# One score product per head from q·exp(L) and k·exp(−L), and the mean of z moved into w_out, in a gated linear recurrence with a feed-forward block

## The chip, the cores and the metric

The kernel runs on one core of a Trainium2 chip. The metric is the time of one execution on the device in microseconds (us). Engine names are those of the profile: PE is TensorE, PEld its weight loads, DVE is VectorE, ACT is ScalarE, POOL is GpSimd, SP issues DMA. PEclk is the clock granted to TensorE, as a share of full speed.

## The reference

Two parts follow each other. The first is a recurrence over 768 tokens for 4 batches and 8 heads of width 48, with a complex decay per token and channel. The second is a feed-forward block on 3072 tokens of width 384, with a hidden width of 1024.

```python
mag = np.sqrt(a_re*a_re + a_im*a_im)
scale = np.minimum(mag, 0.999) / (mag + 1e-06)
ar, ai = a_re*scale, a_im*scale
for t in range(S):                       # state S_re, S_im: 48 x 48 per head
    S_re, S_im = ar*S_re - ai*S_im + k[t] v[t]^T,  ar*S_im + ai*S_re
    y[t] = q[t] @ S_re
# ... y of all heads side by side: x, 3072 x 384
h = x @ w_in                             # 3072 x 1024
solu = h * softmax(h)
ln = (solu - mean(solu)) / sqrt(var(solu) + 1e-06) * g_ln
out = ln @ w_out                         # 3072 x 384
```

## The kernel before

Tokens are worked on in chunks of 128, so there are 24 chunks (6 of each batch). Phases are summed up along the tokens, and q and k are doubled into cosine and sine parts. Each head then has 96 rows and a real state. The magnitudes of the decays are handled level by level: a pair of tokens in a chunk meets at one of seven block sizes, and between two levels q and k are multiplied by their blocks' decays (a "fold"). No magnitude is ever divided by, so any decay is in range.

```python
def score(li):                 # level h of 1, 2, 4, 8, 16 (full width) or 32, 64
    for x in range(H):         # 8 heads, 128 weight columns, 64 moving columns
        nc.tensor.matmul(out=o, lhsT=kt, rhs=right(qt, h), start=True, stop=True)
        # ... levels 32 and 64: small products by block
def fold(li):
    nc.vector.tensor_tensor(out=right(QT, h), in0=right(QT, h), in1=left(pm, 1)..., op=OP.mult)
    nc.gpsimd.tensor_tensor(out=left(KT, h), in0=left(KT, h), in1=right(pm, 1)..., op=OP.mult)
    # ... new block decays; then copy_predicated or ACT copies of the scores into attn
# feed-forward of a chunk: turn_x, up, expo, solu, norm, turn_z, down, store
def norm():
    # ... statistics of z on DVE, rs = (var z + 1e-6 s^2)^-0.5 on POOL
    nc.vector.scalar_tensor_tensor(out=nb, in0=mv[:, 0:1], scalar=-1.0, in1=rs, ...)
    nc.scalar.activation(out=z, in_=z, func=AF.Identity, scale=rs, bias=nb)
```

Preparation (magnitudes, phases, sines) goes by groups of two chunks, beside the attention of the group before and the feed-forward of the one before that.

Of the kernel before, what the change touches and what calls it, by code (L numbers as in the profile page):

```python
# [10 lines left out]
FP = mybir.dt.float32  # L11
I32 = mybir.dt.int32
# [4 lines left out]
PSUM = bass.MemoryType.PSUM  # L17
P = 128

# Adding and subtracting it rounds a float of small magnitude to an integer.  # L20
MAGIC = 12582912.0
# A shade under 2 pi, so that half a turn stays in the range of Sin.
TURN = 6.283185
# The block sizes of the intra-chunk scores: pairs in sibling blocks of each size.
MASKED = (1, 2, 4, 8, 16)
LEVELS = MASKED + (32, 64)


def weave(*streams):
    """Runs lists of steps side by side, each spread over its part (begin, end) of the time."""  # L30
    order = []
    for si, (begin, end, steps) in enumerate(streams):
        n = len(steps)
        for i, step in enumerate(steps):
            order.append((begin + (end - begin) * (i + 0.5) / n, si, i, step))
    for _, _, _, step in sorted(order, key=lambda e: e[:3]):
        step()


def constants(H):  # L40
    """What depends on shapes alone: identity, inclusive prefix sum, last row to all rows, masks."""
    s = np.arange(P)
    last = np.zeros((P, P))
    last[P - 1] = 1.0
    mats = np.concatenate([np.eye(P), np.triu(np.ones((P, P))), last], 1)
    masks = []
    for h in MASKED:
        left = (s // h) % 2 == 0
        own = (s // (2 * h))[:, None] == np.arange(P // (2 * h))[None]
        m = np.broadcast_to((own & left[:, None])[:, None, :, None], (P, H, P // (2 * h), h))  # L50
        masks.append(m.reshape(P, H * P // 2))
    return mats.astype(np.float32), np.concatenate(masks, 1).astype(np.uint8)


@with_exitstack
def kernel(
    ctx: ExitStack,
    tc: tile.TileContext,
    q: bass.AP,
    k: bass.AP,  # L60
    v: bass.AP,
    a_re: bass.AP,
    a_im: bass.AP,
    moe_w_in: bass.AP,
    moe_w_out: bass.AP,
    moe_g_ln: bass.AP,
    out: bass.AP,
):
    """The recurrence over chunks of 128 tokens, with a[t] = m[t] exp(2 pi i phi[t]).

    Phases: with T the running sum of phi, Re(prod a[s+1..t]) = prod m * cos(T[t] - T[s]), so q and k
    are doubled into (cos T, sin T) parts and the state stays real, of 2 D rows.

    Magnitudes are never divided by: a pair s < t of one chunk meets at the one block size h at which
    s and t lie in the left and the right one of two sibling blocks. There q carries the product of m
    from its block's start, k that from behind it to its block's end, both at most 1. From h to 2h,
    right blocks of q and left blocks of k take up the whole product of their sibling.
    """
    nc = tc.nc
    B, H, S, D = q.shape  # L80
    D2 = 2 * D
# [45 lines left out]
    def heads(t):  # L127
        return t.rearrange("p (h d) -> p h d", d=D)

# [1 line left out]
    def load(g):  # L131
        for nm, src, pool in (("ar", a_re, ld), ("ai", a_im, ld), ("q", q, ld), ("k", k, ld), ("v", v, ldv)):
            t = pool.tile([P, G, DM], FP, tag=nm, name=nm)
# [4 lines left out]
            T[nm, g] = t  # L138

    def weight_steps():  # L140
        """The weights come as float64: to float32, rounded to nearest, by their bits. What is under
        float32's normal range goes to (next to) zero. w_out's rows take up g_ln."""
        NW = 512
        steps = []
        for w, src, nk in ((w_in, moe_w_in, KD), (w_out, moe_w_out, KF)):
            wide = src.bitcast(I32).rearrange("(c p) w -> p c w", p=P)
            nf = w.shape[2]
            for c in range(nk):
                for f0 in range(0, nf, NW):
                    steps.append((w, wide, c, f0, min(NW, nf - f0)))  # L150

        def convert(w, wide, c, f0, n):
            def f():
                raw = ffp.tile([P, NW, 2], I32, tag="z", name="raw")[:, 0:n]
                both = zp.tile([P, 2, NW], I32, tag="zT", name="bits")[:, :, 0:n]
                nc.sync.dma_start(out=raw.rearrange("p n u -> p (n u)"), in_=wide[:, c, 2 * f0:2 * (f0 + n)])
                lo, hi, x, y = raw[:, :, 0], raw[:, :, 1], both[:, 0], both[:, 1]
                ts, stt = nc.vector.tensor_scalar, nc.vector.scalar_tensor_tensor
                ts(out=x, in0=hi, scalar1=0x7FFFFFFF, scalar2=None, op0=OP.bitwise_and)
                nc.gpsimd.tensor_tensor(out=x, in0=x, in1=rebias.to_broadcast([P, n]), op=OP.add)  # L160
                ts(out=y, in0=x, scalar1=31, scalar2=-1, op0=OP.arith_shift_right, op1=OP.bitwise_xor)
                stt(out=x, in0=x, scalar=3, in1=y, op0=OP.logical_shift_left, op1=OP.bitwise_and)
                stt(out=x, in0=lo, scalar=29, in1=x, op0=OP.logical_shift_right, op1=OP.bitwise_or)
                stt(out=x, in0=hi, scalar=-2 ** 31, in1=x, op0=OP.bitwise_and, op1=OP.bitwise_or)
                ts(out=y, in0=lo, scalar1=28, scalar2=1, op0=OP.logical_shift_right, op1=OP.bitwise_and)
                nc.gpsimd.tensor_tensor(out=w[:, c, f0:f0 + n].bitcast(I32), in0=x, in1=y, op=OP.add)
                if w is w_out:
                    nc.gpsimd.tensor_scalar(out=w[:, c], in0=w[:, c], scalar1=g_ln[:, c:c + 1], scalar2=None,
                                            op0=OP.mult)
            return f  # L170

        return [convert(*s) for s in steps]

# [1 line left out]
    def prep_steps(g):  # L175
        st = {}

# [12 lines left out]
            nc.gpsimd.tensor_tensor(out=st["t1"], in0=st["t1"], in1=st["t2"], op=OP.add)  # L190

        def s1():
            # Twice |a|: a square root and a Newton step on it.
            t1, t2, t3 = st["t1"], st["t2"], st["t3"]
            nc.scalar.activation(out=t2, in_=t1, func=AF.Sqrt, bias=tiny)
            nc.vector.reciprocal(out=t3, in_=t2)
            nc.gpsimd.tensor_tensor(out=t3, in0=t1, in1=t3, op=OP.mult)
            nc.gpsimd.tensor_tensor(out=t2, in0=t3, in1=t2, op=OP.add)

        def s2():  # L200
            # m = |a| min(|a|, 0.999) / (|a| + 1e-6)
            t1, t2, t3 = st["t1"], st["t2"], st["t3"]
            T["M", g] = nat.tile([P, G * H, 2, D], FP, tag="M", name="M")
            nc.gpsimd.tensor_scalar(out=t1, in0=t2, scalar1=2e-6, scalar2=2.0, op0=OP.add, op1=OP.mult)  # L204
            nc.vector.reciprocal(out=t1, in_=t1)  # L205
            nc.vector.scalar_tensor_tensor(out=t3, in0=t2, scalar=1.998, in1=t2, op0=OP.min, op1=OP.mult)
            nc.gpsimd.tensor_tensor(out=t1, in0=t3, in1=t1, op=OP.mult)
            nc.scalar.copy(out=T["M", g], in_=twice(t1))

        def s3():  # L210
            # tan of half the angle of (|a_re|, a_im), with a_re's sign: a_im / (a_re + copysign(|a|, a_re))
            t1, t2, t3, ar, ai = (st[nm] for nm in ("t1", "t2", "t3", "ar", "ai"))
            nc.vector.scalar_tensor_tensor(
                out=t2.bitcast(I32), in0=ar.bitcast(I32), scalar=-2 ** 31, in1=t2.bitcast(I32),
# [5 lines left out]
            nc.gpsimd.tensor_scalar(out=t1, in0=t1, scalar1=0.0, scalar2=0.5, op0=OP.is_lt, op1=OP.mult)  # L220

        def s4():
            # phi in turns: half a turn more where a_re is negative
            t1, t3, ai = st["t1"], st["t3"], st["ai"]
            nc.scalar.activation(out=t3, in_=ai, func=AF.Arctan, scale=2.0)
            nc.vector.scalar_tensor_tensor(out=t3, in0=t3, scalar=1.0 / math.pi, in1=t1, op0=OP.mult, op1=OP.add)  # L226

        def phase(j):
            # The running phase, in turns about the nearest integer; it goes on from the last chunk's end.
            def f():  # L230
                b, ti = groups[g][j]
                if j == 0:
# [13 lines left out]
            return f  # L246

        def trig():
            # (-cos, sin); q and k both have the minus.
            cs = T["cs", g]  # L250
            for j, (b, _) in enumerate(groups[g]):
                nc.scalar.activation(out=cs[:, j * H:(j + 1) * H, 1], in_=heads(T["f", b]), func=AF.Sin, scale=TURN)
            nc.scalar.activation(out=cs[:, :, 0], in_=cs[:, :, 0], func=AF.Sin, scale=TURN, bias=quarter)

        def own():
            # The pairs s = t: v[t] (q[t] . k[t])
            qk = tmp.tile([P, G * H, D], FP, tag="qk", name="qk")
            dot = sml.tile([P, G * H, 1], FP, tag="dot", name="dot")
            vd = vdp.tile([P, G, DM], FP, tag="vd", name="vd")
# [16 lines left out]
            nc.vector.tensor_tensor(out=T["K", g], in0=T["cs", g], in1=twice(flat(T["k", g])), op=OP.mult)  # L276

        def turn(nm, j, half):
            # Four heads of [tokens, 2 D] to [2 D, tokens]
            def f():  # L280
                pool = trm if nm == "M" else tr
                if half == 0:
# [10 lines left out]
        turns = [turn(nm, j, half) for j in range(G) for nm in ("K", "Q", "M") for half in range(2)]  # L293
        return [s0, s1, s2, s3, s4] + [phase(j) for j in range(G)] + [trig, own, doubled_k, doubled_q] + turns

# [1 line left out]
    def chunk_steps(g, j):  # L297
        b, ti = groups[g][j]
        att = attn[j]
# [98 lines left out]
            steps += [keys(0), keys(1), carry]  # L398
        return steps

# [1 line left out]
    def ffn_steps(g, j):  # L402
        b, ti = groups[g][j]
        st = {}
# [25 lines left out]
            nc.vector.tensor_tensor(out=st["z"], in0=st["h"], in1=st["z"], op=OP.mult)  # L430

        def norm():
            # solu = z / s with s = sum + 1e-9: (solu - mean) / sqrt(var + 1e-6) = (z - mean z) / sqrt(var z + 1e-6 s^2)
            z = st["z"]
            bs = sml.tile([P, FF // 512, 6], FP, tag="bs", name="bs")
            mv = sml.tile([P, 2], FP, tag="mv", name="mv")
# [38 lines left out]

        return [turn_x, up(0), up(1), expo, solu, norm, turn_z(0), turn_z(1), down(0), down(1), store]

# [1 line left out]
    load(0)  # L479
    nc.sync.dma_start(out=mats, in_=nc.inline_tensor(mats_np, name="mats_np").ap().rearrange("p (n t) -> p n t", n=3))  # L480
    nc.sync.dma_start(
# [25 lines left out]
        weave(*streams)  # L507


# [1 line left out]
_INS = ['q', 'k', 'v', 'a_re', 'a_im', 'moe_w_in', 'moe_w_out', 'moe_g_ln']  # L511
_OUTS = [((3072, 384), 'float32')]
# [25 lines left out]
```

## Time and profile before

| | before |
|---|---|
| time, median of 3 | 1291.54 us (1290.56 to 1293.04) |
| profiled span, mean PEclk | 1284.6 us, 0.756 |
| first product with w_out (o) starts | 248.9 us |
| a steady pair of chunks | 99.0 us, of it PE idle 16.0 |

The next lines are the view of waits (waiting engine, operation and line, then the releaser; us in total, times, longest us):

```profile
PE score L317 <- DVE attn L342: 106.8, 23, 23.0
PE zt L457 <- ACT z L448: 76.9, 21, 7.7
```

PE waits 106.8 us for DVE between score levels (57.9 of them before 249 us, in the start; a steady pair of chunks has one such wait of 5.2 us), and 76.9 us, in 21 of the 24 chunks, for the normalised z before it can transpose it. POOL and ACT have longer waits (ACT 211.6 us for nb), but they have time to spare, and a wait of such an engine need not cost anything.

### The profile page before, as it was taken

The numbers are of one execution on the slowest core, as the hardware profiler recorded it, in microseconds if no ns is written. First come the engines' busy times: TensorE is split into PE (matmuls) and PEld (weight loads), VectorE is DVE, ScalarE is ACT, GpSimd is POOL, SyncE is SP. The second block draws the span as 40 slices with busy tenths as digits, with TensorE's granted clock in tenths as the row PEclk, the third lists the DMA queues.
The fourth block names the chain that finished last, engine by engine and source line by source line (L and its number), as shares of the span: only waits on it lengthen the run. The fifth ranks groups of instructions, "written<-read, shape, count | busy, mean of one in ns | idle before, by whom it ended". The sixth has DMA issues, their size and how long they took to land.

```text
span 1284.6 us, 14523 instructions
## 1 busy us (share of the span) xinstructions
PE 991.7 (77%) x5856; PEld 797.0 (62%) x5856; DVE 765.8 (60%) x804; ACT 383.4 (30%) x574; POOL 615.1 (48%) x562
## 2 busy tenths in 40 slices
PE   0058855588978978978988888788788798799976
PEld 0057834466676666666766776676666676677753
DVE  4888777766655665665755754763763773734411
ACT  2232302133324324224323323323322423231121
POOL 5585666555544454464363363463453453434300
PEclk9975565578858868778778678687687687788878
DMA  9332121102102102101101101100100000000000
GB/s 145 80 64 60 38 49 49 25 7 44 31 1 44 31 1 44 31 1 36 39 1 32 38 7 32 37 7 21 37 18 19 1 7 7 1 7 7 7 7 12
DMA packets 131666, 36.06 MB, mean 28 GB/s; under 512 B 126480, under 2 KB 129680, under 8 KB 131600
## 3 DMA queue, kind: packets, MB, share of 16 engines
q1 hardware_dynamic: 131600, 35.14, 12.9%
q8 instruction: 46, 0.75, 0.3%
q14 instruction: 20, 0.16, 0.0%
HBM read 30.41 MB, written 4.72 MB: 27 GB/s over the span
## 4 chain that ended last, share of the span: by engine, by line
PE 59%; DVE 18%; POOL 12%; issue 7%; ACT 3%; DMA 0%; POOLq 0%; SPq 0%; DVEq 0%; ACTq 0%
PE score L317 17%; PE o L466 12%; PE y L359 5%; PE turned L287 4%; PE y L362 4%; DVE t L218 3%; PE zt L457 3%; PE h L418 3%; PE score L321 3%; DVE attn L342 2%; DVE QT L333 2%; DVE t L217 2%; PE d L384 2%; POOL KT L335 2%; PE phase L236 2%
## 5 line engine op out<-in xcount | busy, mean ns | idle before, releaser
L317 PE MATMUL score<-QT,KT 96*128 96x64 f32 x1920 | 315.7, 336 | 111.7 <-DVE attn L342 106.8
L317 PEld LDWEIGHTS score<-QT,KT 96*128 96x128 f32 x1920 | 311.9, 253 | 131.6 <-issue 72.9
L335 POOL TENSOR_TENSOR KT<-KT,tot 96x512 f32<-96x512 f32 x144 | 196.0, 1365 | 313.2 <-PE score L317 261.8
L333 DVE TENSOR_TENSOR QT<-QT,tot 96x512 f32<-96x512 f32 x144 | 122.1, 856 | 71.5 <-PE score L317 71.1
L466 PE MATMUL o<-w_out,zT 128*128 128x384 f32 x384 | 161.1, 564 | 0.0
L418 PE MATMUL h<-w_in,xT 128*128 128x512 f32 x288 | 134.3, 609 | 1.2 <-ACT xT L411 1.2
L342 DVE COPY_PREDICATED attn<-masks,score 128x512 f32<-128x512 uint8 x120 | 112.1, 934 | 0.0
L466 PEld LDWEIGHTS o<-w_out,zT 128*128 128x128 f32 x384 | 82.2, 230 | 45.7 <-issue 17.7
L457 PE MATMUL zt<-mats,z 128*128 128x128 f32 x192 | 46.7, 408 | 76.9 <-ACT z L448 76.9
L338 POOL TENSOR_TENSOR tot<-MT 96x512 f32<-96x512 f32 x24 | 27.0, 1123 | 160.2 <-ACT MT L289 160.2
L359 PE MATMUL y<-v,attn 128*128 128x48 f32 x384 | 95.9, 357 | 1.4 <-issue 1.4
L448 ACT ACTIVATE z<-z,nb,rs 128x1024 f32<-128x1024 f32 x24 | 29.8, 1240 | 211.6 <-DVE nb L447 211.6
L205 DVE RECIPROCAL t<-t 128x768 f32<-128x768 f32 x12 | 59.4, 4951 | 53.6 <-POOL t L204 53.6
L457 PEld LDWEIGHTS zt<-mats,z 128*128 128x128 f32 x192 | 34.0, 209 | 84.1 <-ACT z L448 81.4
L418 PEld LDWEIGHTS h<-w_in,xT 128*128 128x128 f32 x288 | 52.5, 193 | 53.8 <-issue 51.7
L359 PEld LDWEIGHTS y<-v,attn 128*128 128x128 f32 x384 | 83.8, 278 | 2.1 <-issue 1.7
L362 PE MATMUL y<-state,QT 96*128 96x48 f32 x320 | 83.2, 352 | 0.3 <-DVE QT L333 0.2
L391 DVE TENSOR_TENSOR state<-d,state 96x384 f32<-96x384 f32 x16 | 8.9, 554 | 115.9 <-PE d L384 115.9
L321 PE MATMUL score<-QT,KT 96*32 96x32 f32 (+1 forms) x1152 | 49.9, 220 | 30.5 <-DVE QT L333 27.7
L321 PEld LDWEIGHTS score<-QT,KT 96*32 96x32 f32 (+1 forms) x1152 | 45.4, 134 | 43.4 <-issue 36.1
L236 PE MATMUL phase<-t,mats 128*128 128x384 f32 x48 | 36.8, 875 | 45.5 <-DVE t L226 45.5
L362 PEld LDWEIGHTS y<-state,QT 96*128 96x128 f32 x320 | 70.5, 271 | 0.5 <-DVE QT L333 0.4
(93 smaller groups left out, 1647.8 us busy)
## 6 DMA issues: line engine op xcount, KB each, us to landing
ar<-in_a_re_dram SPq DMA_DIRECT2D x24, 192.0 KB, 3.6
ai<-in_a_im_dram SPq DMA_DIRECT2D x24, 192.0 KB, 3.3
q<-in_q_dram SPq DMA_DIRECT2D x24, 192.0 KB, 3.9
k<-in_k_dram SPq DMA_DIRECT2D x24, 192.0 KB, 3.4
v<-in_v_dram SPq DMA_DIRECT2D x24, 192.0 KB, 3.3
out_dram<-ot SPq DMA_DIRECT2D x24, 192.0 KB, 1.9
raw<-in_moe_w_in_dram SPq DMA_DIRECT2D x6, 512.0 KB, 4.3
raw<-in_moe_w_out_dram SPq DMA_DIRECT2D x8, 384.0 KB, 3.0
```

What stands on the lines that cost most here:

```text
L205: nc.vector.reciprocal(out=t1, in_=t1)
L236: nc.tensor.matmul(out=ps, lhsT=tri, rhs=st["t3"][:, j * DM:(j + 1) * DM], start=True, stop=(ti == 0))
L317: nc.tensor.matmul(out=o, lhsT=kt, rhs=right(qt, h), start=True, stop=True)
L321: nc.tensor.matmul(out=o[a:a + h, h * y:h * (y + 1)], lhsT=kt[:, a:a + h], rhs=qt[:, a + h:a + 2 * h], start=True, stop=True)
L333: nc.vector.tensor_tensor(out=right(QT, h), in0=right(QT, h), in1=left(pm, 1).to_broadcast([D2, n, h]), op=OP.mult)
L335: nc.gpsimd.tensor_tensor(out=left(KT, h), in0=left(KT, h), in1=right(pm, 1).to_broadcast([D2, n, h]), op=OP.mult)
L342: nc.vector.copy_predicated(right(att, h), masks[:, li].rearrange("p (x i) -> p x i", i=h), ps.rearrange("p (x i) -> p x i", i=h),)
L359: nc.tensor.matmul(out=ys, lhsT=att[:, x * P:(x + 1) * P], rhs=V[:, x * D:(x + 1) * D], start=True, stop=(ti == 0))
L362: nc.tensor.matmul(out=ys, lhsT=T["QT", g, j][:, x * P:(x + 1) * P], rhs=state[b][:, x * D:(x + 1) * D], start=False, stop=True)
L418: nc.tensor.matmul(out=st["h"][:, half * 512:(half + 1) * 512], lhsT=st["xT"][:, c * P:(c + 1) * P], rhs=w_in[:, c, half * 512:(half + 1) ...
L457: nc.tensor.transpose(out=ps[:, i * P:(i + 1) * P], in_=st["z"][:, c * P:(c + 1) * P], identity=ident)
L466: nc.tensor.matmul(out=st["o"], lhsT=st["zT"][:, c * P:(c + 1) * P], rhs=w_out[:, c], start=(c == 0), stop=(c == KF - 1))
```

## The change

The intent: with L the running sum of log-magnitudes inside a chunk, the decay between tokens s and t is exp(L[t]) · exp(−L[s]). So q takes exp(L), k takes exp(−L), and one product of 128 by 128 per head gives all scores of a chunk, to be masked once. This only works if exp(−L) stays in range. The kernel therefore collects three checks (on the angles, the size of the inputs and the end decays), and a branch at the end runs the old level-by-level way (now the function `general`) if one fails. The feed-forward block changes too. Subtracting the mean of z before the product with w_out is the same as subtracting from w_out the mean of each of its columns, and the factor rs can be applied to the output. So the normalising pass over z goes away, and the statistics run beside the transposes. Preparation now takes all four batches at once, and ACT's order of instructions is fixed by the program.

```diff
+def whole(ctx, tc, flag, q, k, v, ...):
+            nc.scalar.activation(out=up, in_=st["lr"], func=AF.Exp)                # exp(L)
+            nc.scalar.activation(out=dn, in_=st["lr"], func=AF.Exp, scale=-1.0)    # exp(-L)
+            nc.sync.dma_start(out=T["ends", ti], in_=up[P - 1:P, :])               # end decays
+            for nm, t in (("q", up), ("k", dn)):
+                nc.gpsimd.tensor_tensor(out=x, in0=x, in1=t, op=OP.mult)
 ...
+        def score(half):                    # replaces 7 levels of score and fold
+                for i in range(4):
+                    nc.tensor.matmul(out=ps[:, i], lhsT=KT[:, x * P:(x + 1) * P],
+                                     rhs=QT[:, x * P:(x + 1) * P], start=True, stop=True)
+                nc.vector.tensor_tensor(out=st["att"][...], in0=ps, in1=tri..., op=OP.mult)
 ...
+        def centre():                       # w_out minus the mean of its columns
+            for c in range(KF):
+                nc.tensor.matmul(out=ps, lhsT=ones, rhs=w_out[:, c], ...)
+            for c in range(KF):
+                nc.vector.scalar_tensor_tensor(out=w_out[:, c], in0=ps, scalar=-1.0 / FF,
+                                               in1=w_out[:, c], op0=OP.mult, op1=OP.add)
 ...
-        return [turn_x, up(0), up(1), expo, solu, norm, turn_z(0), turn_z(1), down(0), down(1), store]
+        return [turn_x, up(0), up(1), expo, solu, turn_z(0), turn_z(1), norm, down(0), down(1), store]
 ...
+        inner.enter_context(tc.manual_schedule(engines={mybir.EngineType.Activation}))
+        whole(inner, tc, flag, *args)
+    needed = nc.values_load(flag[0:1, 0:1])
+    with tc.If(needed != 0, name="general"):
+            general(inner, tc, *args)
```

## The prediction

> **What bounds the kernel now.** I read the page's busy shares, the 40 slices and the chain that ended last first.
>
> ```profile
> PE   991.7 (77%) x5856; PEld 797.0 (62%) x5856; DVE 765.8 (60%) x804; ACT 383.4 (30%) x574; POOL 615.1 (48%) x562
> PE   0058855588978978978988888788788798799976
> PEclk9975565578858868778778678687687687788878
> PE 59%; DVE 18%; POOL 12%; issue 7%; ACT 3%; DMA 0%; POOLq 0%; SPq 0%; DVEq 0%; ACTq 0%
> ```
>
> (In order: busy us, share and instructions of each engine; TensorE by slice; its clock by slice; the chain by engine.) TensorE is busy 77% of 1284.6 us, but only at a granted clock that swings; its mean is 0.756 in the core view. The chain is mostly PE, with DVE and POOL steps between. Groups by line show what a score costs:
>
> ```profile
> L317 PE MATMUL score<-QT,KT 96*128 96x64 f32 x1920 | 315.7, 336 | 111.7 <-DVE attn L342 106.8
> L335 POOL TENSOR_TENSOR KT<-KT,tot 96x512 f32<-96x512 f32 x144 | 196.0, 1365 | 313.2 <-PE score L317 261.8
> L333 DVE TENSOR_TENSOR QT<-QT,tot 96x512 f32<-96x512 f32 x144 | 122.1, 856 | 71.5 <-PE score L317 71.1
> L342 DVE COPY_PREDICATED attn<-masks,score 128x512 f32<-128x512 uint8 x120 | 112.1, 934 | 0.0
> ```
>
> Five full-width score levels per chunk, and between levels q and k are folded on DVE and POOL, each side waiting for the other. Next the chain in order of time, around 660 us:
>
> ```profile
> 659.20 0.22 PE y L362 x2
> ...
> 666.73 0.43 PE y L362 x2
> ```
>
> The same y product (two instructions) takes 0.22 us, then 0.43. Short windows over that place carry the granted clock in the column before the last two:
>
> ```profile
> 642.00:648.00 6.00, 6.00 (x81) 3.42 (x80) 0.00 (x0) 2.58 (x7) 5.83 (x5) 1.00 0.00 0
> 668.00:672.00 4.00, 4.00 (x21) 4.00 (x20) 0.00 (x0) 0.00 (x0) 1.39 (x6) 0.50 0.00 0
> 672.00:676.00 4.00, 0.27 (x2) 0.11 (x1) 2.57 (x3) 0.55 (x1) 2.97 (x4) 0.50 0.00 0
> 680.00:684.00 4.00, 4.00 (x18) 2.90 (x17) 0.00 (x0) 1.81 (x4) 0.00 (x0) 0.68 0.01 4
> ```
>
> So the clock is full or half. It falls after idle stretches, and also in an unbroken run of y products, whose 48 moving columns against 128 weight columns keep the array little used (668 to 672). It recovers a few us into work of wide moving operands.
>
> **What the skill says.** "TensorE: Matmul & The Clock Gate", Part 1, says the clock is half or full, set by activity in free-running windows of about 3.4 us. The trace agrees on the two levels (0.50 and 1.00 above); idle gaps of about 4 us precede the half clock. Its "LDWEIGHTS" section says a weight load costs by its columns: a y product with 48 moving columns takes 0.22 us at full clock, and h with 512 takes 0.86 (six in 5.14 us at 1237 us), four times as much, not ten, so the trace agrees that narrow products pay for their 128 weight columns. "SBUF — State Buffer", "SBUF: two separate sides", says a DVE operation with two SBUF inputs or in a two-port mode and a GpSimd operation exclude each other for the whole instruction. The trace agrees: the DVE's add at L217 takes 0.96 us alone, median 3.07, and this DVE mask of 384 elements (mean 0.42 us) ends only when POOL's multiply of 58.74 to 60.60 does:
>
> ```profile
> 58.87 1.95 DVE L243 TENSOR_SCALAR cs<-f 128x384 int32<-128x384 int32 x1
> 58.74 1.86 POOL L198 TENSOR_TENSOR t<-t,t 128x768 f32<-128x768 f32 x1
> ```
>
> "ScalarE: Activation LUTs", "What ACT_TABLE_LOAD costs", gives about 1283 ns for a load; the groups show 54 loads of 1283 ns each. The new kernel has 13 in its order of instructions, 53 us of ACT less, off the path.
>
> **TensorE work, part by part,** at full clock for one chunk of one batch. Durations are read where the clock is 1.00: narrow product with 128 weight columns 0.22 us, d (96 weights) 0.165, transpose 0.11 (kt 0.083), h 0.86, o and phase 0.64.
>
> Before: score 5 x 8 x 0.22 = 8.8; the two small levels about 1.6; M's transposes 8 x 0.11 = 0.9; k's way back (kt) 0.7; K and Q transposes 1.8; y 16 x 0.22 = 3.5; d 1.3; x, z transposes 1.2; h 5.1; o 5.1; phase 1.3. Sum 31.3; 24 chunks 751 us; divided by 0.756 that is 993, against 991.7 measured busy. The table holds.
>
> After: scores become 8 products of 128 by 128, priced as the narrow one since the weights are the same 128 columns: 1.8. M and kt go. The prefix sum of log m adds a 0.64. Sum 21.75 us, 522 us for 24 chunks: 31% less.
>
> **The other engines.** DVE loses the folds (122 + 32), the predicated copies (112) and three reciprocals per group (178). It gains per group of four chunks (elements 1536, rates of the same forms in the trace): two two-input operations 1.75 each in the phase part, the maximum 1.7, the clamp 1.0, two for log m 3.5, four evacuations 2.2, phases 6.0, eight doublings 7.6, small ones 0.6: about 26 us, or 6.5 per chunk. Per chunk 7.3 remain (mask 1.4, x 0.55, state 0.55, max 1.2, product 1.2, statistics 1.9, store 0.55). So 13.8 a chunk; with the float64 weights (about 63) and the centring (8 x 0.56), 400 us instead of 766. POOL: 13 us a group plus 1.6 a chunk plus weights 48: about 160 instead of 615. ACT: ten activations of 1.48 per group, sines 3.8, loads, and 5.3 a chunk: about 255. All below PE's 21.75 per chunk, so PE should become the bound, if it is fed.
>
> The mean's move into w_out takes the normalising pass on z (1.24 us, waiting 211.6 us in all on DVE's nb) off the z-to-transposes path. The last chunk shows it: product ends 1246.1, transposes begin 1250.1. 4 us a chunk of latency go; only what was not hidden counts, so I do not add 24 x 4.
>
> **Start.** The order of instructions has the new preparation serial for all four batches: ar lands at about 7 us, maximum, Ln, Exp, POOL multiply 3.6 (twice L219's 1.8), four steps to atan's argument (21), log m (32), prefix sums (38), exponentials (41). PE's next instruction is a transpose of the chunk's end decays, which come by a DMA and a POOL copy queued behind two POOL multiplies of 3.6 each: 50. Phases to 57, sines and doubling to 69. Then 11 of 14 weight conversions (DVE 4 to 5 us each, 49 in all) lie in the same queue with the next preparation's 9, scores and the mean's centring. First o at about 148 us. Before, it was at 248.9, so 100 us come from here.
>
> **Steady state.** By batch within a group, PE at full clock needs 19.6, 22.2, 24.7, 19.6 us. I walked each queue. In batch 0, the next preparation's POOL multiply keeps the DVE (lock), which delays the row maximum and the second mask; ACT's squares stand before z's evacuation: about 30. In batch 1 the end-decay transpose waits behind POOL again, some 4 us of idle PE and half clock after: 29. In batch 2, phases, five sines and the table load stand before the exponential: 31. Batch 3 fits: 21. Sum 111, or 27.7 per chunk, a factor 1.29 over full clock.
>
> First o 148 + rest of its chunk 6 + 18 chunks x 27.7 (499) + last four without preparation 4 x 20 (80) + the last feed-forward alone 21 (before: about 23, 4 less latency, colder clock) + flag load and branch, a guess of 4 = 758 us. The run's time is 7 over the profile's span before (1291.5 against 1284.6): 765. Because my waits may overlap more than walked, I set 760.
>
> **Rivals.** (1) PE runs unbroken and stays at full clock: 18 chunks x 22.5 = 405 saves 94, about 670. For it: DVE and POOL have half idle. Against: y and d stretches without wide products did drop the clock at 668 us. (2) The inefficiency of before stays: there 49 us per chunk between 249 and 1225 us (976 us for about 20 chunks), 1.57 over its 31.3; then 34 per chunk, 18 x 34 = 612, about 875. For it: in-order queues with one-buffered loads and two PSUM buffers for all turns, and clock loss that feeds itself. Against: the level-by-level ping-pong of PE with DVE and POOL, the cause of the longest waits (POOL on score 278.7 us), is gone. (3) DVE or ACT becomes the bound: ACT's order is fixed by the program and may hold evacuations of turns behind sines; then batches 0 to 2 cost 35 to 40 and the time is 850 to 900. (4) The flag comes out set and the old way runs too: about 2000. Computed from the inputs, products of |a| over 128 tokens stay near exp(-13), far over 1e-18, angles' fourth powers sum under 0.9 where 5 is allowed: out of the question but for an error.
>
> **Range and chances.** Rival 1 gives the low edge, with a little of its gain missing: 690. Halfway to rivals 2 and 3 gives the high edge: 835. No rival but the fourth reaches 1265, so faster 0.98, same 0.01, slower 0.01.
>
> **What would show it.** PE busy about 520 divided by the granted clock, 610 to 660 us; clock 0.80 to 0.88; DVE near 400, POOL near 165, ACT near 255. Score: 384 instructions near 0.11 us each of path at full clock. First o near 148. PE idle before the end-decay transpose, four times some 4 us, released by POOL. If scores by 128 moving columns cost over 0.22 us each, or the clock stays at 0.75, or first o comes past 180, the prediction is wrong there; also if the longest PE waits are on ACT.

## The result, and the profile after

The changed kernel is correct and took **752.81 us** (median of four, 743.38 to 755.11) against 1291.05 for the kernel before on the same chip. Two of the four executions, 755.11 and 754.77, count as slow; the fast ones took 743.38 and 750.85. The ratio of the fast runs is **0.5786** (95% interval 0.5754 to 0.5819). A ratio is the mean time of one kernel's fast runs over that of the other's of the same rounds, so it is not quite the ratio of the medians quoted. A later set of six executions of the same kernel gave 746.02 us and a ratio of 0.5768.

The page of the profiled execution (span 741.6 us, mean PEclk 0.878), its busy shares and the slices of PE and its clock:

```profile
PE 588.8 (79%) x2887; PEld 416.1 (56%) x2887; DVE 380.3 (51%) x590; ACT 246.4 (33%) x325; POOL 171.3 (23%) x133
...
PE   0215217768998988998988989898989989999994
...
PEclk9955658669996999998989999989989999999997
```

PE is busy 588.8 us instead of 991.7, and its clock is mostly full after the first quarter. What stands out instead is the start: in the first six slices, up to 111 us, PE does little. The new score's group by line (instructions; busy us, mean ns of one; idle time before):

```profile
L768 PE MATMUL f_score<-f_qT,f_kT 96*128 96x128 f32 x384 | 56.9, 283 | 0.0
```

The score is now 384 instructions and 56.9 us, where the five wide levels alone took 315.7. (Each product of two float32 operands is two instructions: 24 chunks x 8 heads x 2 = 384.) What PE still waits for, in the view of waits:

```profile
PE f_L L659 <- DVE f_lr L652: 32.6, 1, 32.6
PE f_tot L684 <- POOL f_e L682: 27.3, 5, 10.4
PE f_mean L611 <- POOL f_w_out L604: 26.8, 7, 13.5
```

The waits for the prefix sum (f_L) and for the weights (f_mean) lie wholly in the start. So do two of the five waits for the end decays (f_tot), 10.4 and 6.3 us. The other three, in the steady state, are 3.5 us each.

The same four chunks repeat through the middle. Cut at the transposes of x, one steady group reads as follows in the view of stretches (start and end; us; then busy us and instructions of PE, PEld, DVE, ACT, POOL; then PEclk, DMA share, GB/s):

```profile
428.80:456.40 27.60, 24.02 (x121) 18.12 (x120) 13.92 (x17) 15.38 (x18) 6.86 (x5) 0.88 0.18 36
456.40:485.50 29.10, 25.59 (x130) 18.75 (x130) 11.32 (x20) 7.87 (x12) 8.58 (x6) 0.89 0.32 66
485.50:514.30 28.80, 26.28 (x136) 18.29 (x135) 20.49 (x35) 12.43 (x18) 6.24 (x4) 0.99 0.07 14
514.30:534.60 20.30, 20.30 (x119) 14.91 (x119) 7.69 (x13) 4.95 (x10) 1.15 (x3) 1.00 0.40 74
```

Batch 3, last, has PE busy in all of its 20.3 us at full clock. The other three have 2.5 to 3.6 us of idle PE each, and batches 0 and 1 pay for it once more by a clock of 0.88 and 0.89.

The gap in batch 0, seen from DVE in order of time (start us, us, engine, line, operation; in brackets the idle time before it and its releaser):

```profile
436.39 1.76 DVE L636 TENSOR_TENSOR f_x<-f_ar,f_x 128x1536 f32<-128x1536 f32 x1 [5.61 <-POOL f_ai L635]
438.07 1.22 DVE L832 TENSOR_REDUCE f_nmax<-f_h 128x1 f32<-128x1024 f32 x1
439.20 1.75 DVE L637 SCALAR_TENSOR_TENSOR f_x<-f_x,f_ai 128x1536 f32<-128x1536 f32 x1
440.87 0.68 DVE L770 TENSOR_TENSOR f_att<-f_score,f_mats 128x512 f32<-128x512 f32 x1
```

The preparation's POOL product (L635, from 432.93, 3.43 us) reads f_x until 436.36. The DVE product (L636) writes over that tile, so it has waited by a semaphore: of its 5.61 us the last 3.5, since the Exp that both need ended only at 432.85. Behind it in DVE's queue stand the row maximum (L832), the next preparation step (L637) and the second mask (L770). PE needs that mask for y and starts it at 441.61 after 3.57 us of idle time. The gap in batch 1, seen from POOL:

```profile
472.75 3.44 POOL L672 TENSOR_TENSOR f_q<-f_q,f_ar 128x1536 f32<-128x1536 f32 x1
476.15 3.42 POOL L672 TENSOR_TENSOR f_k<-f_k,f_ai 128x1536 f32<-128x1536 f32 x1
479.51 0.25 POOL L682 COPY f_e<-f_ends 32x96 f32<-32x96 f32 x1
```

A copy of 0.25 us stands behind two POOL products of 3.4 us each. PE's next instruction, the transpose of the end decays, needs it and starts at 479.82 after 3.51 us. The gap in batch 2, seen from ACT:

```profile
500.20 1.56 ACT L718 ACTIVATE f_cs<-f_cs,f_bias 128x1536 f32<-128x1536 f32 x1
501.78 1.28 ACT L719 ACT_TABLE_LOAD   x1
503.08 1.11 ACT L833 ACTIVATE f_z<-f_h,f_nmax 128x1024 f32<-128x1024 f32 x1
```

The row maximum that the exponential (L833) needs was done at 502.23. The exponential starts 0.85 us later, when the table load behind the sine has ended. The product of z follows at 504.34, and PE has idled 1.31 us when it starts z's transposes at 505.61. It had idled 0.96 us before that for the evacuation of y.

### The profile page after: what moved, and what is told of

Read it like the earlier page. It is cut to its first block, busy times and chain, and to the rows that moved or that the text cites. A ratio compares the mean times of both kernels' runs of the same rounds, so it can differ in the third digit from the quotient of the medians.

```text
span 741.6 us, 7378 instructions
## 1 busy us (share of the span) xinstructions
PE 588.8 (79%) x2887; PEld 416.1 (56%) x2887; DVE 380.3 (51%) x590; ACT 246.4 (33%) x325; POOL 171.3 (23%) x133
## 5 line engine op out<-in xcount | busy, mean ns | idle before, releaser
L870 PE MATMUL f_o<-f_w_out,f_zT 128*128 128x384 f32 x384 | 139.8, 512 | 0.0
L824 PE MATMUL f_h<-f_w_in,f_xT 128*128 128x512 f32 x288 | 130.8, 597 | 0.6 <-ACT f_xT L817 0.6
L870 PEld LDWEIGHTS f_o<-f_w_out,f_zT 128*128 128x128 f32 x384 | 74.4, 204 | 44.0 <-issue 7.0
L824 PEld LDWEIGHTS f_h<-f_w_in,f_xT 128*128 128x128 f32 x288 | 53.2, 190 | 58.8 <-issue 51.7
L779 PE MATMUL f_y<-f_v,f_att 128*128 128x48 f32 x384 | 73.2, 285 | 14.6 <-DVE f_att L770 14.5
L833 ACT ACTIVATE f_z<-f_h,f_nmax 128x1024 f32<-128x1024 f32 x24 | 26.7, 1113 | 148.0 <-DVE f_nmax L832 125.3
L779 PEld LDWEIGHTS f_y<-f_v,f_att 128*128 128x128 f32 x384 | 61.1, 204 | 19.7 <-DVE f_att L770 15.4
L782 PE MATMUL f_y<-f_state,f_qT 96*128 96x48 f32 x320 | 65.9, 290 | 0.0
L832 DVE TENSOR_REDUCE f_nmax<-f_h 128x1 f32<-128x1024 f32 x24 | 29.3, 1223 | 60.0 <-PE f_h L824 60.0
L768 PEld LDWEIGHTS f_score<-f_qT,f_kT 96*128 96x128 f32 x384 | 53.2, 201 | 9.3 <-issue 6.8
L768 PE MATMUL f_score<-f_qT,f_kT 96*128 96x128 f32 x384 | 56.9, 283 | 0.0
L782 PEld LDWEIGHTS f_y<-f_state,f_qT 96*128 96x128 f32 x320 | 52.7, 206 | 0.0
L770 DVE TENSOR_TENSOR f_att<-f_score,f_mats 128x512 f32<-128x512 f32 x48 | 32.9, 685 | 28.5 <-PE f_score L768 28.5
```

The source lines that it names most:

```text
L768: nc.tensor.matmul(out=ps[:, i], lhsT=KT[:, x * P:(x + 1) * P], rhs=QT[:, x * P:(x + 1) * P], start=True, stop=True)
L770: nc.vector.tensor_tensor(out=st["att"][:, half * 4:half * 4 + 4], in0=ps, in1=tri.unsqueeze(1).to_broadcast([P, 4, P]), op=OP.mult)
L779: nc.tensor.matmul(out=ys, lhsT=st["att"][:, x], rhs=V[:, x * D:(x + 1) * D], start=True, stop=(ti == 0))
L782: nc.tensor.matmul(out=ys, lhsT=T["qT", ti, b][:, x * P:(x + 1) * P], rhs=state[b][:, x * D:(x + 1) * D], start=False, stop=True)
L824: nc.tensor.matmul(out=st["h"][:, half * 512:(half + 1) * 512], lhsT=st["xT"][:, c * P:(c + 1) * P], rhs=w_in[:, c, half * 512:(half + 1) ...
L832: nc.vector.tensor_reduce(out=nmax, in_=st["h"], op=OP.max, axis=AX.X, negate=True)
```

## The experiments

All variants are correct unless it is said otherwise. Ratios are against the kernel before.

**1. The mean alone (before_mean).** The kernel before with only the mean's move into w_out.

```diff
-            nc.vector.scalar_tensor_tensor(out=nb, ...)
-            nc.scalar.activation(out=z, in_=z, func=AF.Identity, scale=rs, bias=nb)
+        def centre(): ...        # as in the change, once, after the weights
-        ... expo, solu, norm, turn_z(0), turn_z(1), down(0), ...
+        ... expo, solu, turn_z(0), turn_z(1), norm, down(0), ...
```

> The kernel before with nothing changed but the mean put into w_out, so that the normalising pass over z goes and the factor is applied to the output. Theory (z's path shortened by about 4 us a chunk, and TensorE's 77 us of waiting for the normalised z mostly goes): 1200 to 1240 us. Rival (the latency was hidden, since TensorE has scores to do meanwhile): within 15 us of the kernel before, 1276 to 1306.

Measured: 1157.74 us, ratio 0.896 (0.8913 to 0.9008), so some 134 us less, more than expected. A steady pair of chunks in the kernel before, then here:

```profile
690.60:789.70 99.10, 83.10 (x505) 67.14 (x504) 59.53 (x61) 32.70 (x49) 47.25 (x44) 0.76 0.12 25
```

```profile
636.10:721.50 85.40, 76.14 (x505) 61.69 (x504) 59.76 (x61) 29.62 (x45) 47.50 (x44) 0.82 0.14 29
```

The same 505 PE instructions take 85.4 us instead of 99.1. PE's idle time falls by 6.7 us (99.1 − 83.1 = 16.0 to 85.4 − 76.1 = 9.3). Its busy time falls by 7.0 us for the same work, because the granted clock rises from 0.76 to 0.82. Half of the gain of a latency removed is thus the wait itself, and the other half is the clock.

**2. One product per head alone (before_one_score).** The kernel before with one product of 128 by 128 per head, no folds and no magnitudes' transposes. It is wrong on purpose: the decays' magnitudes are left out of q and k.

```diff
-        for li in range(len(LEVELS)):
-            steps += [score(li), fold(li)]
+        steps = [score(0), score(1), values]     # 4 heads each, then one mask on DVE
```

> The kernel before with its own preparation and pairing of batches, but one 128 by 128 product per head instead of the seven levels, no folds and no transposes of M. Wrong on purpose: the decays are left out. Theory (the levels and their exchange with VectorE and GpSimd are most of the cost; TensorE per chunk falls from 31.3 to about 21.8 us at full clock, VectorE from 766 to about 530 us in all): 850 to 930 us, three quarters of the whole gain. Rival (preparation in fours, the scalar engine's fixed order and the shorter start are as large a part): 1000 to 1100 us.

Measured: 996.74 us, ratio 0.7723. This is less of a gain than the theory's 850 to 930, and just under the rival's 1000 to 1100. PE's work fell as planned (636.3 us busy), but the view of waits shows a wait that grew in its place:

```profile
PE zt L421 <- ACT z L412: 164.1, 13, 35.7
```

In the kernel before, the same wait was 76.9 us, at most 7.7 at a time. Here it is 35.7 us once in the start and 13.5 to 14.7 us once in each of seven steady pairs of chunks. One of these, in order of time:

```profile
602.07 4.94 DVE L218 RECIPROCAL t<-t 128x768 f32<-128x768 f32 x1
608.99 2.78 POOL L220 TENSOR_SCALAR t<-t 128x768 f32<-128x768 f32 x1
612.53 1.24 ACT L412 ACTIVATE z<-z,nb,rs 128x1024 f32<-128x1024 f32 x1 [2.77 <-DVE nb L411]
```

The product of z was done at 599.19, and PE starts the transposes at 613.82. The normalising pass is only 1.24 us of that. A reciprocal of the preparation (L218) stands before the variance on DVE, and two operations of the preparation (L219 from 607.09, L220) stand before rs on POOL. So what stands open with the attention short is z's whole path through the statistics, with the preparation in its queues.

**3. The mean taken back (znorm_back).** The changed kernel with the normalising pass back on z (the centring of w_out is kept, which is harmless).

```diff
+            nc.vector.scalar_tensor_tensor(out=nb, in0=mv[:, 0:1], scalar=-1.0, in1=st["rs"], ...)
+            nc.scalar.activation(out=z, in_=z, func=AF.Identity, scale=st["rs"], bias=nb)
-        ... solu, turn_z(0), turn_z(1), norm, ...
+        ... solu, norm, turn_z(0), turn_z(1), ...
```

> The changed kernel with the normalising pass over z put back between the product and the transposes, w_out still centred (the result stays right). Theory (in the changed kernel z becomes ready just as TensorE is done with the y products, so 4 us more of latency stand open in each of 24 chunks, and the clock falls in them): 830 to 870 us, TensorE waiting for z some 70 to 100 us. Rival (hidden behind other products): at most 765.

Measured: 892.63 us, ratio 0.6915. By the ratios the loss is some 146 us, far above the expectation.

```profile
PE f_zt L845 <- ACT f_z L866: 115.8, 24, 7.8
```

All 24 chunks wait, 4.8 us each, and the mean clock falls from 0.878 to 0.794. In a steady group of four chunks (133.3 us against 105.8), PE idle time grows by 17.9 us and busy time for the same work by 9.6 us.

**4. ACT's order left to the scheduler (act_auto).**

```diff
-        inner.enter_context(tc.manual_schedule(engines={mybir.EngineType.Activation}))
```

> The changed kernel without the fixed program order of the scalar engine: the order of instructions then has about 89 table loads instead of 13, 98 us more on that engine, part of it ahead of the exponential and the evacuations. Theory (the fixed order is worth something): 780 to 830 us. Rival (the scalar engine at 33% has room, and a freer order fills waits): 735 to 760.

Measured: 740.28 us, ratio 0.5739 (0.5721 to 0.5757). The theory that the order is needed falls, and the rival is right. ACT loads tables 70 times instead of 13, and its busy time goes from 246.4 to 319.8 us. None of it reaches the end. The steady group is 105.7 us, as before. First o comes at 163.9 us instead of 156.9 and the eighth chunk at 332.3 instead of 323.0, and yet the end is no later: the last four chunks with preparation take 94.3 us instead of 102.3.

**5. The product's own place (x0_own).** The DVE product that waited in batch 0 is written over another tile, so that it need not wait for POOL's reading.

```diff
-            nc.vector.tensor_tensor(out=x0, in0=ar, in1=x0, op=OP.mult)
-            nc.vector.scalar_tensor_tensor(out=x0, in0=x0, scalar=2.0, in1=ai, ...)
+            nc.vector.tensor_tensor(out=ar, in0=ar, in1=x0, op=OP.mult)
+            nc.vector.scalar_tensor_tensor(out=x0, in0=ar, scalar=2.0, in1=ai, ...)
```

> The changed kernel with the VectorE product of the angle's argument written over a_re's tile instead of over x0, which GpSimd still reads. In the changed kernel VectorE stands 5.6 us there in each group, by a semaphore. Theory (it is this wait for a tile, not the shared port, that delays the row maximum and the second mask and costs TensorE 3.6 us a group and clock after it): the wait goes, the product takes under 2.5 us beside GpSimd, 725 to 742 us. Rival (my predicted reason, the port that both engines share): the product then itself takes about 5 us beside GpSimd's 3.4 us multiply, and the time stays within 745 to 756.

Measured: 757.94 us, ratio 0.5872: no gain, and somewhat slower. The timeline of the same place shows why:

```profile
439.37 1.76 DVE L636 TENSOR_TENSOR f_ar<-f_ar,f_x 128x1536 f32<-128x1536 f32 x1 [2.10 <-ACT f_x L630]
439.41 5.00 POOL L635 TENSOR_TENSOR f_ai<-f_ai,f_x 128x1536 f32<-128x1536 f32 x1 [3.71 <-ACT f_x L630]
446.12 1.22 DVE L832 TENSOR_REDUCE f_nmax<-f_h 128x1 f32<-128x1024 f32 x1
448.12 0.68 DVE L770 TENSOR_TENSOR f_att<-f_score,f_mats 128x512 f32<-128x512 f32 x1
```

The DVE product now starts as soon as the Exp has ended. But POOL's product, issued 0.04 us after it, takes 5.00 us instead of 3.43. It ends at 444.41, 3.28 us after the DVE product's end at 441.13. The two thus ran one after the other. The Trainium skill states this ("SBUF — State Buffer", section "SBUF: two separate sides"): a DVE operation with two SBUF inputs and a GpSimd operation that reads SBUF exclude each other for the whole instruction. The trace agrees. The semaphore went and the exclusion took its place: the two products are done 5.08 us after the end of the Exp, against 5.30 in the changed kernel. The next DVE operation (L637) needs POOL's result and waits 3.33 us, until 444.45. DVE's order of instructions changed with the edit, too. The row maximum (L832) stood before L637 and now stands behind it, and one more step of the preparation (L638) now stands before the second mask (L770). The mask is later than before (PE's gap before y is 4.34 us instead of 3.57). How much of the loss is due to this order was not separated. The theory's 725 to 742 us thus failed. The rival's exclusion is there, but it lengthens POOL's operation and not DVE's, and the time is above the rival's 745 to 756.

**6. The end decays without POOL (ends_dma).** They are fetched twice by DMA instead of once with a POOL copy.

```diff
-            nc.sync.dma_start(out=T["ends", ti], in_=up[P - 1:P, :])
+            for u in range(2):
+                nc.sync.dma_start(out=T["ends", ti][:, u], in_=up[P - 1:P, :])
-            nc.gpsimd.tensor_copy(out=e2, in_=e.unsqueeze(1).to_broadcast([B * H, 2, D]))
```

> The changed kernel with the end decays fetched twice by DMA, so that GpSimd's copy, which stands behind its two multiplies of 3.4 us, goes. Theory (the transpose of the end decays, first in TensorE's queue after o, costs 3.5 us in each of three groups and 6 to 10 us twice in the start, with clock lost after it): TensorE's wait falls from 27 to under 8 us, 720 to 740 us. Rival (the DMA lands too late or another wait comes in its place): 745 to 756.

Measured: 737.58 us, ratio 0.5725 (0.5708 to 0.5742), within the theory's 720 to 740.

```profile
PE f_tot L683 <- DMA f_ends<-f_ar: 7.3, 2, 4.8
```

POOL's 27.3 us are gone and 7.3 remain, in the start. Batch 1 of a steady group falls from 29.1 to 23.45 us at full clock. But batches 0 and 2 go from 27.5 and 28.8 us to 28.7–30.1 and 29.6–31.2. Their idle time is the same or smaller, and their clock is lower (0.77 to 0.94). The group of four takes 103.0 us against 105.8, so that in this execution half of the 5.6 us that batch 1 gave was lost again to the clock next door.

**7. Each score twice (score_twice).** It asks whether PE's work still sets the pace.

```diff
+                    for _ in range(2):
                         nc.tensor.matmul(out=ps[:, i], lhsT=KT[...], rhs=QT[...], start=True, stop=True)
```

> The changed kernel with each score product done twice (same result). TensorE gets 8 x 0.22 = 1.76 us more per chunk at full clock, 42 us in all. Theory (TensorE sets the pace in most of the span): 780 to 800 us, and the added products take 0.22 us each at full clock. Rival (TensorE waits for others, and the clock is higher with more wide products): under 765.

Measured: 772.75 us, ratio 0.599 (0.5978 to 0.6002), so 26 to 29 us more than the changed kernel's two sets by the ratios, between theory and rival. The group by line:

```profile
L769 PE MATMUL f_score<-f_qT,f_kT 96*128 96x128 f32 x768 | 98.8, 275 | 0.0
```

That is 41.9 us more of score in PE's busy time. In the steady state the cost is one to one: the 16 chunks from the fourth to the nineteenth, cut at the transposes of x, take 448.5 against 420.1 us, 28.4 more, where they have 16 x 1.76 = 28.2 of score (23.8 more than in experiment 9, whose clock was lower). Up to the fourth chunk it costs nothing (209.9 us against 216.8): there PE waits for others.

**8. No branch (no_branch).** The load of the flag and the branch with the old way are left out.

```diff
-    needed = nc.values_load(flag[0:1, 0:1])
-    with tc.If(needed != 0, name="general"): ...
```

> The changed kernel without the load of the flag and without the branch with the old way in it. Theory (the branch costs a few us at the end): 3 to 7 us less. Rival (hidden in the tail): within 2 us.

Measured: 743.73 us, ratio 0.5762 (0.5752 to 0.5772).

**9. The changed kernel again (after_again).** It has no edit.

> The changed kernel once more, unaltered, as the yardstick for what the smaller edits brought. Theory: its executions spread from 743 to 755 us by the clock they are granted and nothing else, so on this chip it comes to 740 to 750 (ratio 0.574 to 0.582) and the version without branch (743.7, ratio 0.576) is no faster: the branch costs under 1 us. Rival: the branch and the load of its flag cost 3 to 4 us, then this run stays at a ratio of 0.578 to 0.580 or more with an interval that lies above 0.5772.

Measured: 746.02 us (741.92 to 754.9), ratio 0.5768 (0.5752 to 0.5783). The interval overlaps that of the version without a branch almost fully, so the branch's cost is not to be told from zero. The two ratios differ by 0.0006 of 1291 us, which is 0.8 us. There is more to learn from the spread. In this execution the transpose of x of the eighth chunk came at 323.0 us, as in the first profile. The next group of four then took 109.0 us instead of 105.8, with the same idle time of PE (9.4 and 9.6 us) and a lower clock in three of its four chunks. The group after that took 106.0 us. The same program with the same waits gets a different clock. In the clock records of the two traces it falls at the same place (335.88 and 335.89 us, after the same gap of PE), and stays at half for 6.83 us in the first and for 10.24 us here. The Trainium skill says that the clock's windows run freely and do not start with the kernel ("TensorE: Matmul & The Clock Gate", section "Part 1: The HAM clock gate"). The records agree that there are windows: in all 14 traces each whole stretch at one clock lasts a multiple of 3.41 us. But they don't explain this difference, since the windows lie at the same place in both executions. Why one took a window more at half clock is open. So differences of a few us between variants of this kernel mean little from single executions.

**10. A shorter start (start_both).** The factor g_ln goes into the centring step and off POOL, and the weights are converted beside the first preparation.

```diff
-                    nc.gpsimd.tensor_scalar(out=w[:, c], in0=w[:, c], scalar1=g_ln[:, c:c + 1], ...)
-                nc.tensor.matmul(out=ps, lhsT=ones, rhs=w_out[:, c], ...)
+                nc.tensor.matmul(out=ps, lhsT=means[:, c], rhs=w_out[:, c], ...)   # -g_ln / FF
-            nc.vector.scalar_tensor_tensor(out=w_out[:, c], in0=ps, scalar=-1.0 / FF, in1=w_out[:, c], ...)
+            nc.vector.scalar_tensor_tensor(out=w_out[:, c], in0=w_out[:, c], scalar=g_ln[:, c:c + 1], in1=ps, ...)
-    for f in sum(prep_steps(0), []) + turn_steps(0, 0):
-        f()
+    weave((0.0, 0.6, sum(prep_steps(0), []) + turn_steps(0, 0)), (0.0, 1.0, weight_steps()))
```

(The cut leaves out eight POOL operations that make `means` once, at the beginning.)

> The changed kernel with two edits of its start alone: the factor g_ln goes into the centring step of w_out, so that 8 operations of POOL of 1.59 us fall away, and the weights are converted beside the first preparation instead of after it. Theory: the start is a chain of DVE and POOL in which PE only waits (first o at 157 us in a span of 742); 13 us of POOL and some 10 to 15 us of waiting for the weights fall away, first o comes at 135 to 145 us and the time is 720 to 733. Rival: DVE's own work up to the first chunk is the bound and only changes its order, first o stays within 5 us of 157 and the time is 740 to 752.

Measured: 737.28 us, ratio 0.5714 (0.5702 to 0.5726). First o came at 137.5 us, where the theory put it, but the time lies between the theory's 720 to 733 and the rival's 740 to 752. Of 19.4 us at the first o, 11.0 are left at the eighth chunk (312.0 against 323.0 us). The profiled group after it took 111.1 us against 105.8, with 9.4 us of idle PE against 9.6, so that again only the clock differs.

**11 and 12. Start and end decays together, with ACT's order fixed (best_fixed) and free (best_auto).** The edits of 6 and 10, then those of 4 too.

> The two edits of the start together with the end decays fetched twice by DMA. Theory: start and steady state are different stretches, so the gains add: 13 to 20 us from the start and about 10 from the end decays, 712 to 726 us. Rival: what one wait gives the others take by the clock, and it is no better than the better of the two alone, 730 to 740.

> The same with ACT's order left to the scheduler. Theory: ACT's order was worth nothing by itself (740 against 743), so within 5 us of the version with the fixed order. Rival: with the start shortened, ACT's many more table loads (some 89 against 13) lie on the path there, and it is 8 us or more slower than the fixed order.

Measured: best_fixed 725.27 us, ratio 0.5613 (0.5599 to 0.5626), in the range of the theory, so these gains do add. By the ratios to the changed kernel's 0.5768 the start alone brought 7.0 us, the end decays alone 5.6 and both 20.0. That is more than the sum, and why was not tested. best_auto took **714.46 us** (711.99 to 723.9, the latter a slow run), ratio 0.5560 (0.5528 to 0.5592). This is better than either side expected, and 3.6% below the changed kernel on the same chip (0.5560 / 0.5768). In its expectation I wrote 89 table loads; the trace has 70. A steady group of it:

```profile
408.80:429.10 20.30, 20.28 (x121) 14.91 (x120) 6.92 (x12) 6.31 (x11) 1.20 (x3) 1.00 0.04 16
429.10:452.80 23.70, 23.27 (x129) 16.29 (x129) 12.48 (x20) 7.85 (x12) 8.64 (x6) 1.00 0.33 55
452.80:484.60 31.80, 29.31 (x136) 20.99 (x136) 24.43 (x38) 17.80 (x22) 11.21 (x5) 0.84 0.18 38
484.60:511.50 26.90, 23.14 (x119) 16.57 (x119) 11.21 (x16) 18.92 (x21) 1.56 (x3) 0.87 0.41 74
```

Two of four chunks now run at full clock almost without idle time. This group has PE at 96.0 us of work in 102.7, where best_fixed has 100.9 in 107.0 at a lower clock. The largest difference lies behind it: the last four chunks with preparation take 94.1 us, with PE idle for 0.7, against 105.8 with 6.0 idle, which is 11.7 of the 14.6 us between the two spans. act_auto has the same short group (94.3), but a later start. Why the free order fits these edits better was not tested.

## Why the prediction was right or wrong

The time (760 predicted, 752.81 measured) and the range (690 to 835) held. That the number came so near is in part luck: the start was 12 us longer and the steady state 28 us shorter than predicted. By its own sum, with the cuts at the transposes of x in the profiled run:

| term | predicted | measured |
|---|---|---|
| to the end of the chunk with the first o | 148 + 6 = 154 | 166.1 |
| 18 chunks with preparation | 499 (27.7 each) | 470.8 (26.2 each) |
| four without | 80 | 78.6 |
| last feed-forward, flag, branch | 21 + 4 | 26.1 |
| span | 758 | 741.6 |
| run over span | 7 | 1.8 |

**TensorE's work by parts: right.** 522 us at full clock over the measured 0.878 is 594, against 588.8 busy. The 610 to 660 named at the prediction's end were missed on the low side: they answer to clocks of 0.85 to 0.79, and the clock came out at the upper end of its own range (0.80 to 0.88). A score instruction costs 0.109 us of path, as said (41.9 us for 384 more in experiment 7). DVE 380.3 (400 predicted), ACT 246.4 (255) and POOL 171.3 (165) came near too. Experiment 7 shows that PE paces the steady state. One reading of the clock was misplaced: the half clock shown from 668 to 672 us began at 662.05, and the idle stretch shown (672 to 676) came after that. The rule drawn from it holds all the same, as PE had no idle time from 654.31 to 672.27 and did almost only y products in the 3.41 us before the fall.

**The start: 9 us short.** First o came at 156.9 us instead of 148. The mis-sized term is the weights: "DVE 4 to 5 us each, 49 in all" for 11 of them. It counted DVE's time, but a tile goes back and forth between DVE and POOL. The POOL additions that end the eight tiles of w_out start from 100.4 to 144.3 us, 6.3 us apart on average, and 5.1 where least stands between them (three from 121.0 to 131.2). DVE works 2.7 us on such a tile, by the sum of its six operations' medians. Moving that multiply and weaving the conversion in earlier took 19.4 us off the first o (experiment 10). Which of the two edits brought how much was not separated.

**The steady state: 106 instead of 111 us a group.** By batch, 30/29/31/21 were predicted and 27.5/29.1/28.8/20.3 measured. Batch 1 was right in cause and size: 3.5 us of idle PE for the end decays behind POOL's products, as stated (some 4), and experiment 6 shows it. What failed is the count: four such waits were predicted, and the trace has five, of which the two in the start are longer. In batch 0 the named mechanism failed. The prediction put the delay of the row maximum and the mask down to the lock between POOL and DVE, but in the trace the DVE operation waits by a semaphore for a tile that POOL reads. Experiment 5 shows that the lock was not far: with the semaphore gone, it holds POOL's product for some 1.6 us (5.00 instead of 3.43), and the pair of products ends hardly earlier. Batch 2 was right in cause in part, by the trace alone: the table load before the exponential costs 0.85 us of the 2.5 us that PE idled, and 0.96 went to a wait for y's evacuation that was not named. It was 2 us too high in size, as the clock stayed at 0.99.

**The mean: left out of the sum.** "Only what was not hidden counts, so I do not add 24 x 4" was a sound caution for the sum, since the steady state was walked with z's short path already in it. As a statement of the part's worth it said too little. The part is worth 134 us alone and 146 us in the changed kernel (experiments 1 and 3), more than 24 x 4 = 96, because each open wait also takes clock: 7.0 us of the 13.7 in a pair of the kernel before.

**The parts are not a sum.** The mean alone brings 134 us, one product per head alone 294 (an upper bound, since the decays' own work is left out), and together they would make 428. The change brought some 545 (0.4214 to 0.4232 of 1291). The rest must come with the preparation in groups of four, the shorter start and the way the parts open each other's waits. These were not separated by a run. First o comes 92 us earlier in the changed kernel (156.9 against 248.9), but only 10.6 us earlier with the mean alone and 47.3 with one product alone.

**The last terms.** A run over its span is 1.8 us, not 7. The kernel before has 1.8 as well where both numbers are of one execution (1286.51 and 1284.7). The prediction had subtracted the span of one execution from the median of others. The branch, guessed at 4, is not measurable.

**The rivals.** Full clock throughout (670) did not come. The inefficiency of before (875) did not persist: 26.2 us over the average need of 21.5 (a quarter of 19.6 + 22.2 + 24.7 + 19.6) is 1.22, not 1.57. ACT and DVE are no bounds.

## What to carry to other kernels

When an engine's work falls by a third, look for the latencies that the old work had hidden, and take them away in the same change. Here a pass over z of 1.24 us, with the statistics that it waits for, was worth over 130 us, a third to a half of it through the clock (9.6 of 27.5 us in a group of experiment 3, 7.0 of 13.7 in a pair of experiment 1). Before removing a semaphore wait between DVE and POOL, check whether the two operations would exclude each other anyway. Judge variants that differ by a few us only by many executions, since the same program with the same waits got a different clock.

## What the Trainium skill lacked or had wrong

- "TensorE: Matmul & The Clock Gate" has no duration for products of float32 operands. Each is two instructions here. An h product with 512 moving columns takes 0.86 us at full clock (eight instructions in 3.60 us, 0.43 to 0.45 each), four times the 215.7 ns that the page measures at this width for its own case. Its section "LDWEIGHTS" gives columns / 1.2 ns, 107 ns for 128 columns. As a rate this holds at full clock (a y product, with two such loads, every 0.22 us); a single load beside h is recorded as 190 ns.
- The same page, Part 1, says for modelling that "the ramp penalty is <1% of a typical kernel span". This is said of the ramp alone and is no budget for the clock. Here the clock fell 18 times, the mean granted clock was 0.878 and PE was busy 588.8 us for work that needs about 522 at full clock (the prediction's table): some 67 us of 741.6, or 9%. It also does not mention that the clock falls in an unbroken run of narrow products. In the kernel before, 15 of 40 falls follow 3.41 us in which PE was busy for 99% or more, mostly with y products of 48 or scores of 64 moving columns (the fall at 662.05 us is one).
- "ScalarE: Activation LUTs", section "What ACT_TABLE_LOAD costs": 1283 ns agrees, but the total of 2.66 us for a switch does not show. In batch 2 the exponential starts at 503.08, 1.32 us after the end of the sine before the load. 57 more loads (70 against 13) raised ACT's busy time by 73.4 us, 1.29 each, and the kernel got no slower.
- "Runtime: NRT & Kernel Launch", section "Instruction fetch mechanics", calls runtime control flow expensive and gives no figure. One flag load and one branch at the end cost nothing that can be told apart here (ratios 0.5768 with, 0.5762 without). By the intervals a cost of up to some 3 us could hide, so this does not contradict the page.
